# Linear attention and a gated feed-forward layer in one kernel: numerators, cosines, W sums, v casts and x transposes at other places in a hand-written order

## Chip, cores and metric

The kernel runs on one core of a Trainium2 chip. The metric is the device time of one execution in microseconds (us); before the change the median of three runs is 320.25 us (317.77 to 322.56). Five engines work side by side, each through its own list of instructions in order: TensorE (PE; its weight loads are listed as PEld), VectorE (DVE), ScalarE (ACT), GpSimd (POOL) and SyncE (SP). SP does nothing here but issue DMA transfers. An instruction waits on semaphores for the data and buffers that it needs, and everything behind it on the same engine waits with it.

## The reference

```python
batch, n_heads, seq, head_dim = 8, 8, 576, 64
theta = pi / 2 * arange(seq) / seq
def phi(x):                       # 64 -> 128 features
    r = maximum(x, 0)
    return concatenate([r * cos(theta), r * sin(theta)], axis=-1)
kv  = einsum('bhsf,bhsd->bhfd', phi(k), v)
z   = phi(k).sum(axis=2)
num = einsum('bhsf,bhfd->bhsd', phi(q), kv)
den = einsum('bhsf,bhf->bhs', phi(q), z)[..., None] + 1e-6
x   = (num / den).transpose(0, 2, 1, 3).reshape(4608, 512)
out = (gelu(x @ w_gate) * (x @ w_val)) @ w_out     # 512 -> 1536 -> 512
```

## The kernel before, in words

The attention works on batches b = 0 to 7 (576 tokens each, 4.5 tiles of 128), the feed-forward layer on blocks n = 0 to 8 of 512 tokens. The two are laid into each other: while PE multiplies block n, the attention of batch n+1 is finished and batch n+2 is loaded and prepared. The scheduler of the framework is switched off (`manual_schedule`), so each engine runs its instructions in the order in which the Python code emits them. Semaphores follow from the regions of tiles that are read and written.

**Attention of a batch.** q, k and v come from DRAM as fp32 into `st`, three slots of which q and k take the first two (`stage`, L84). For the late batches each of q and k comes in two loads: j = 0 to 3, and j = 4 to 8 (`LOADS`, L915; j counts nine groups of tokens). A *prep* makes relu(x) times cosine or sine for one j as bf16 into `phis`: `prep` for one of q, k; `prep_both` (L183) for both at once, on DVE or on ACT. `cast_v` (L207) turns v into bf16 in `vx`. `turn_q` (L220) transposes phi(q) with two DMA transposes issued from SP into the single tile `qT`, so it has to wait until the last numerators of the batch before have read `qT`. `kv_unit` (L264) multiplies phi(k) with v. `nm_unit` (L309), the *numerators* of a tile t of 128 tokens, are eight PE matmuls from `qT` into PSUM banks 6 and 7, and three DVE steps (L322 denominator, L323 reciprocal, L324 product) that write `x_sb`. `turn_x` (L375) transposes `x_sb` into `xT` of a block, again by DMA from SP.

**Feed-forward.** Blocks 0 to 3 use plain matmuls: `gv_unit` (L420) makes gate and value of 128 of the 1536 columns in PSUM, ACT takes the gelu (L439), DVE the product (L442) into `hT`. From block 4 on, gate and value are made with seven products instead of eight (class `Pair`, L639). These need sums of weights S1 to S4 (`w_sum`, L609, into `ws`) and sums of x, T1 to T4 (`x_sum`, L618, on POOL). In blocks 4 and 5 a `group` (L700) makes one `Pair` and one `gv_unit`; from block 6 on `fast_step` (L721) runs a new pair and the end of the pair before. In a `Pair`, in the order of a group:

- `p1`: four + four matmuls of 128x256 into the bank `sum`; ACT copies it to the bank `other` (L669), which must be free of the pair before (its L695).
- `p5`: into bank 3 (`MIX`); ACT copies it (L673).
- `p6`: goes on in `sum`; it has to wait for L669. DVE adds (L677) into `MIX`.
- `p2`: into `other`, then a gelu (L682). `p3`: into `MIX`, then a gelu (L686).
- `p7`: goes on in `sum`; DVE adds (L690) and multiplies (L691).
- `p4`: goes on in `sum`, which L690 must have read; DVE multiplies (L695).

The output product of block n-1 runs beside block n in one step per slot: `o_step` (L963) emits one or two of seven `product`s (L538) of six matmuls each, with copies on ACT (L565), sums on DVE (L560), and the sums of h on DVE or POOL (`h_sum`, L529). Finished rows are collected in `stores` and issued on SP by `flush` (L455), at every third step and inside `product`.

**What sets the order around the change.** Three places:

1. The list `order` (L855) between blocks 0 and 1, with its entries `("w", ...)` for the sums S2 and S4.
2. The loop over n = 1 to 3 and the steps jt = 0 to 11 (L982). In a step come: gate and value, the output step with its stores, turns of x, numerators, the preps and casts of `COMING` (L901), loads, and further sums.
3. Blocks 4 to 8, where `slot(n, jt)` (L1097) emits the output step, then `attention(n, jt)` (L1071), then the sums of `MORE`. A group g of blocks 4 and 5 holds slots 3g, 3g+1 and 3g+2: the first between p5 and p6, the second between p2 and p3, the third inside the `gv_unit`, between its gate half and p4. `PREPS` (L1059) says which preps of batch n+2 go into which slot: a letter c or C for cosine and s for sine, a capital for DVE, else ACT, and the digit j. `numerators` (L1065) says in which slots of block n the tiles of batch n+1 come; it is called after p1, after p6 and, with the third slot, ahead of p4.

On SP the end of block 3 emits `turn_q(5)`, and slot (4, 0) emits the loads of j = 4 to 8 of q and k of batch 6 behind it. In the same way slot (4, 11) emits `turn_q(6)`, and slot (5, 0) the second halves for batch 7.

## Time and profile before

The profiled execution took 318.62 us; its span from the first to the last instruction is 316.8 us. TensorE's granted clock was 0.999 on average.

| | before |
|---|---|
| median of 3 runs | 320.25 us (317.77 to 322.56) |
| profiled execution, span | 318.62 us, 316.8 us |
| PE first product of block 4, of block 5, of block 6 | 150.37, 181.91, 215.45 us |
| POOL busy, 50 to 140 us | 0.00 us |
| PE busy, 130 to 140 us | 7.88 of 10 us |
| DMA transposes of q on SP (`turn_q`), six pairs from 63.70 to 218.15 us | 8.15 to 9.15 us of issue each |
| v cast of 128x1152, DVE and POOL | 0.78 and 1.24 us (mean) |
| cosine prep of q and k together on DVE, shortest and longest | 0.47 and 1.95 us |
| sine or cosine prep of q and k together on ACT | 0.72 us (median) |
| W sum of 128x1024 on DVE | 0.68 us |

How to read it: rows of the timeline give the start in us from the beginning of the span, the duration, the engine (a q behind the name means its sequencer: issuing a transfer, not computing), the line of the kernel, the operation, what is written and read, the shape and the count of instructions in the row; in brackets, how long the engine sat idle before it and what ended that. Rows of waits give who waited for whom, the us in total, how often, and the longest. Busy is a share of the span. A busy PE is not a PE at its peak: a matmul of 128x512 shows as about 0.38 us, while the next one starts 0.216 us after it.

### The profile page before, as it was taken

The numbers are of one execution on the slowest core, as the hardware profiler recorded it, in microseconds if no ns is written. First come the engines' busy times: TensorE is split into PE (matmuls) and PEld (weight loads), VectorE is DVE, ScalarE is ACT, GpSimd is POOL, SyncE is SP. The second block draws the span as 40 slices with busy tenths as digits, with TensorE's granted clock in tenths as the row PEclk, the third lists the DMA queues.
The fourth block names the chain that finished last, engine by engine and source line by source line (L and its number), as shares of the span: only waits on it lengthen the run. The fifth ranks groups of instructions, "written<-read, shape, count | busy, mean of one in ns | idle before, by whom it ended". The sixth has DMA issues, their size and how long they took to land.

```text
span 316.8 us, 7876 instructions
## 1 busy us (share of the span) xinstructions
PE 300.1 (95%) x3055; PEld 223.2 (70%) x3055; DVE 236.8 (75%) x513; ACT 189.5 (60%) x395; POOL 135.7 (43%) x116
## 2 busy tenths in 40 slices
PE   8799998999999999979999989999999999999994
PEld 3574455645876678645777767777889888888883
DVE  5755896899898897669578856996678877757782
ACT  7764774965464754178576748674645555565631
POOL 6675440000000000007865568655994587097420
PEclk9999999999999999999999999999999999999999
DMA  7999999974699979996799899536941403113035
GB/s 269 239 177 235 319 307 397 286 107 70 185 225 182 307 220 133 298 318 176 115 211 275 246 210 168 172 66 80 153 90 37 85 10 68 33 35 66 2 75 127
DMA packets 71125, 53.66 MB, mean 169 GB/s; under 512 B 45392, under 2 KB 58448, under 8 KB 71088
## 3 DMA queue, kind: packets, MB, share of 16 engines
q1 hardware_dynamic: 61312, 41.17, 56.3%
q0 software_dynamic: 9696, 11.93, 16.5%
q8 instruction: 24, 0.39, 0.5%
q14 instruction: 13, 0.11, 0.1%
q10 hardware_dynamic: 80, 0.07, 0.1%
HBM read 37.75 MB, written 9.44 MB: 149 GB/s over the span
## 4 chain that ended last, share of the span: by engine, by line
PE 49%; DMA 24%; DVE 10%; ACT 6%; issue 6%; POOL 1%; SPq 1%; POOLq 0%; ACTq 0%; DVEq 0%
PE ps L650 18%; PE ps L547 14%; PE ps L430 13%; DMA st<-in_q_dram 6%; DMA qT<-phis 5%; DMA wo_sb<-in_moe_w_out_dram 4%; DMA wg_sb<-in_moe_w_gate_dram 2%; DMA st<-in_v_dram 2%; DMA xT<-x_sb 2%; DVE x_sb L324 2%; PE ps L270 2%; DMA wv_sb<-in_moe_w_val_dram 2%; PE ps L311 2%; DVE ps L690 2%; DVE hT L691 2%
## 5 line engine op out<-in xcount | busy, mean ns | idle before, releaser
L430 PE MATMUL ps<-xT,wg_sb 128*128 128x512 bf16 (+1 forms) x256 | 57.2, 346 | 0.7 <-DMA xT<-x_sb 0.5
L430 PE MATMUL ps<-xT,wv_sb 128*128 128x512 bf16 (+1 forms) x256 | 57.2, 346 | 0.3 <-DVE hT L442 0.3
L630 POOL TENSOR_TENSOR fs<-xT 128x512 bf16<-128x512 bf16 x10 | 12.2, 1225 | 98.9 <-DVE x_sb L324 98.0
L439 ACT ACTIVATE gel<-ps 128x512 f32<-128x512 f32 (+1 forms) x64 | 33.8, 530 | 26.6 <-PE ps L430 24.2
L442 DVE TENSOR_TENSOR hT<-gel,ps 128x512 bf16<-128x512 f32 (+1 forms) x64 | 38.0, 601 | 14.5 <-PE ps L430 12.7
L529 POOL TENSOR_TENSOR sm<-hT 128x768 bf16<-128x768 bf16 x20 | 32.8, 1641 | 30.3 <-PE ps L650 15.3
L430 PEld LDWEIGHTS <-wv_sb 128*128 128x128 bf16 x256 | 25.0, 98 | 20.6 <-issue 0.5
L547 PEld LDWEIGHTS <-sm 128*128 128x128 bf16 x336 | 32.7, 98 | 6.3
L650 PE MATMUL ps<-fs,ws 128*128 128x256 bf16 x240 | 34.6, 273 | 2.4 <-ACT ps L669 2.4
L650 PEld LDWEIGHTS <-ws 128*128 128x128 bf16 x320 | 30.5, 98 | 7.9 <-ACT ps L669 2.5
L560 DVE TENSOR_TENSOR o_sb<-sm,ps 128x256 f32<-128x256 f32 x56 | 23.4, 417 | 14.8 <-ACT sm L565 14.1
L177 ACT ACTIVATE phis<-st,sin_t 128x256 bf16<-128x256 f32 (+1 forms) x75 | 31.5, 484 | 4.6 <-DMA st<-in_q_dram 3.8
L430 PEld LDWEIGHTS <-wg_sb 128*128 128x128 bf16 x256 | 23.4, 98 | 15.3 <-DMA xT<-x_sb 0.7
L690 DVE TENSOR_TENSOR ps<-fs,ps 128x512 f32<-128x512 f32 x26 | 18.1, 695 | 19.4 <-PE ps L650 14.0
L650 PE MATMUL ps<-xT,wg_sb 128*128 128x256 bf16 x208 | 31.2, 273 | 0.0
L547 PEld LDWEIGHTS <-hT 128*128 128x128 bf16 x288 | 27.9, 98 | 4.5
L682 ACT ACTIVATE gel<-ps 128x512 f32<-128x512 f32 x26 | 15.5, 597 | 24.6 <-PE ps L650 24.5
L324 DVE TENSOR_TENSOR x_sb<-ps,rec 128x512 bf16<-128x512 f32 x38 | 26.3, 692 | 1.3
L565 ACT COPY sm<-ps 128x256 f32<-128x256 f32 x42 | 15.6, 372 | 16.2 <-PE ps L547 15.8
L547 PE MATMUL ps<-wo_sb,hT 128*128 128x256 bf16 x192 | 23.7, 273 | 0.0
L547 PE MATMUL ps<-wo_sb,sm 128*128 128x256 bf16 x168 | 22.9, 273 | 0.0
L547 PE MATMUL ps<-T,sm 128*128 128x256 bf16 x168 | 22.9, 273 | 0.0
(123 smaller groups left out, 561.7 us busy)
## 6 DMA issues: line engine op xcount, KB each, us to landing
out_dram<-o_sb SPq DMA_DIRECT2D x69, 128.0 KB, 2.5
st<-in_v_dram SPq DMA_DIRECT2D x12, 576.0 KB, 7.6
st<-in_k_dram SPq DMA_DIRECT2D x8, 576.0 KB, 5.0
st<-in_q_dram POOLq DMA_DIRECT2D x4, 576.0 KB, 12.3
st<-in_q_dram SPq DMA_DIRECT2D x4, 576.0 KB, 6.0
st<-in_q_dram SPq DMA_DIRECT2D x3, 640.0 KB, 4.5
st<-in_q_dram SPq DMA_DIRECT2D x3, 512.0 KB, 4.0
wg_sb<-in_moe_w_gate_dram POOLq DMA_DIRECT2D x6, 256.0 KB, 7.3
```

The lines of the kernel that those rows point to most:

```text
L177: nc.scalar.activation(o, i, AF.Relu, scale=tab[:, j:j + 1])
L324: nc.vector.tensor_tensor(x, nm[:, :, :, 0:D], rec[:, :, :, None].to_broadcast([128, 2, 4, D]), op=ALU.mult,)
L430: nc.tensor.matmul(bank(to[g])[:, 0:w], lhsT=wt[:, ct, js], rhs=xt[:, ct, c0:c0 + w], start=(ct == 0), stop=(ct == CT - 1),)
L439: nc.scalar.activation(gel[:, 0:w], bank(to[0])[:, 0:w], AF.Gelu)
L442: nc.vector.tensor_mul(hT[n][:, jt, c0:c0 + w], gel[:, 0:w], bank(to[1])[:, 0:w])
L529: eng.tensor_tensor(a[name][:, j0:j1], a[x][:, j0:j1], a[y][:, j0:j1], op=op)
L547: nc.tensor.matmul(at, lhsT=hs.setdefault(key, h_parts(n, p))[a][:, j], rhs=ts[b][:, j], start=(j == 0 and i in ((1, 2, 4, 5), (1, 4, 5))[ ...
L560: nc.vector.tensor_tensor(o, got[key, k], x, op=op)
L565: nc.scalar.copy(got[key, k], of)
L650: nc.tensor.matmul(to[:, 256 * half:256 * half + 256], lhsT=w_part(a, j * 128, (j + 1) * 128)[:, ct], rhs=xb[self.n][b][:, ct], start=(hal ...
L682: nc.scalar.activation(self.gel0, self.other, AF.Gelu)
L690: nc.vector.tensor_tensor(bank(val), self.m5, self.sum, op=ALU.add)
```

## The change

It computes the same and moves work. In the order of the code:

- Group 0 of blocks 4 and 5 emits, behind its `gv_unit`, the preps of a new slot 12.
- The W sums S2 and S4 (four halves, DVE) leave the list between blocks 0 and 1 and go to steps 3 to 6 of block 3.
- k of batch 5 is loaded in step (2, 10) instead of (2, 11), so ahead of `turn_q(4)`. The preps of q and k of batch 5 begin in step 7 of block 3 instead of 5 and end in step 11 instead of 10.
- In blocks 2 and 3, `turn_x` comes ahead of the output step and its stores.
- The v casts of blocks 2 and 3 go from DVE to POOL.
- `PREPS`: all cosines on DVE now lie in slot 4 (C2, C3, C4) and slot 12 (C0, C1); C5, C7 and C8 of before become c5, c7 and c8 on ACT.
- `numerators`: slots 6, 7, 9, 10 and slot 0 of the next block, in place of 5, 7, 8, 10, 11. They then lie after p1 or after p6 alone. Those of batch 7 begin two slots later.
- `turn_q(6)` and `turn_q(7)` go from slot 11 to slot 0 of the next block, behind the last numerators of the batch before and their turn, and ahead of that slot's loads.

```diff
         gv_unit(n, 8 + g, to=(2, 2), between=between)
+        if g == 0:
+            preps(n, 12)
...
-        + [("q8", 2), ("o", 1, 4), ("w", "S2", 0), ("o", 2, 4), ("kv",), ("q2", 0, 2)]
-        + [("o", 3, 4), ("w", "S2", 512)]
+        + [("q8", 2), ("o", 1, 4), ("o", 2, 4), ("kv",), ("q2", 0, 2)]
+        + [("o", 3, 4)]
...
-        + [("q2", 2, 3), ("w", "S4", 0), ("o", 2, 8), ("xt", 1, 5), ("nm", 3, 6), ("q2", 3, 4)]
-        + [("w", "S4", 512), ("o", 3, 8)]
+        + [("q2", 2, 3), ("o", 2, 8), ("xt", 1, 5), ("nm", 3, 6), ("q2", 3, 4)]
+        + [("o", 3, 8)]
...
-            5: [("qk", 5, js(0, 1))], 6: [("qk", 5, js(1, 2))], 7: [("qk", 5, js(2, 4))],
-            8: [("v", 5, 0), ("qk", 5, js(4, 5))], 9: [("v", 5, 2), ("qk", 5, js(5, 7))],
-            10: [("qk", 5, js(7, 9))],
+            7: [("qk", 5, js(0, 2))], 8: [("v", 5, 0), ("qk", 5, js(2, 4))],
+            9: [("v", 5, 2), ("qk", 5, js(4, 6))], 10: [("qk", 5, js(6, 8))],
+            11: [("qk", 5, js(8, 9))],
...
-        (2, 11): [(5, "k")], (3, 0): [(5, "q")], (3, 1): [(5, "v")],
+        (2, 10): [(5, "k")], (3, 0): [(5, "q")], (3, 1): [(5, "v")],
...
+            i = jt - t_nm - 1
+            if n > 1 and 0 <= i < late_of(b):
+                turn_x(b, i)
             if n > 1:
                 o_step(n, jt)
...
-
-            i = jt - t_nm - 1
-            if n > 1 and 0 <= i < late_of(b):
-                turn_x(b, i)
...
-                    cast_v(c, what, what + 2, dve_copy)
+                    cast_v(c, what, what + 2, nc.gpsimd.tensor_copy)
...
+            if n == 3 and 3 <= jt < 7:
+                w_sum(("S2", "S2", "S4", "S4")[jt - 3], (1 - jt % 2) * 512, (2 - jt % 2) * 512)
...
-        2: "s0 c0", 3: "s1", 4: "C1", 5: "s2 c2", 6: "s3 C3", 7: "s4", 8: "c4 s5",
-        9: "C5 s6", 10: "c6", 11: "s7 C7 s8 C8",
+        2: "s0 s1", 3: "s2", 4: "C2 C3 C4", 5: "s3 s4", 6: "c5", 7: "s5",
+        8: "c6 s6", 9: "s7", 10: "c7", 11: "s8 c8", 12: "C0 C1",
...
+    def preps(n, jt):
+        b = n + 1
+        if 4 <= b < B - 1:
+            for what in PREPS.get(jt, "").split():
+                eng = nc.vector if what[0] == "C" else nc.scalar
+                prep_both(b + 1, "cs".index(what[0].lower()), int(what[1]), eng)
+
     def numerators(n, jt):
-        b, t = n + 1, {5: 0, 7: 1, 8: 2, 10: 3, 11: 4}.get(jt)
-        if t is not None:
+        b, t = n + 1, {6: 0, 7: 1, 9: 2, 10: 3, 0: 4}.get(jt)
+        if jt == 0:
+            b = n
+        if t is not None and b > 4:
             nm_unit(b, t)
             turns.append((b, t))
...
         if n > 5:
-            i, b = n * JT + jt - 6 * JT - 5, B - 1
+            if (n, jt) == (6, 0):
+                numerators(n, jt)
+            i, b = n * JT + jt - 6 * JT - 7, B - 1
...
         b = n + 1
+        if jt == 0 and 5 < b < B:
+            turn_q(b)
...
-            if jt == 11:
-                turn_q(b + 1)
```

## The prediction

> **What bounds the kernel now.** I read the page first, then the two views of waits, then the timeline from 38 to 250 us. The page's busy list says that TensorE (PE) is the bound:

> ```profile
> PE 300.1 (95%) x3055; PEld 223.2 (70%) x3055; DVE 236.8 (75%) x513; ACT 189.5 (60%) x395; POOL 135.7 (43%) x116
> ```

> Its work is the same after the change, so only its idle stretches can be won. Busy time hides part of them, since a matmul counts as busy until its modelled end. I therefore take a gap from starts: the next start, minus the start of the group before it, minus its count times the undisturbed spacing (0.216 us for 512 columns, 0.109 for 256). Example: six matmuls of 256 from 136.83 leave PE free at 137.49, the next starts at 139.77, a gap of 2.28. After 50 us the gaps are (place, us): 52.21 1.56; 57.56 0.18; 74.34 0.39; 113.95 0.71; 120.56 0.49; 137.49 2.28; 147.69 0.31; 151.25 0.39; 164.60 0.31; 167.74 0.52; 183.43 1.12; 197.52 0.31; 200.66 0.52; 210.88 0.62; 216.97 0.68; 229.99 0.81. Together 11.2 us: no edit after 50 us can bring more.

> The largest, in the timeline, with the wait behind it:

> ```profile
> 135.95 0.72 ACT L191 ACTIVATE phis<-st,sin_t 128x512 bf16<-128x512 f32 x1 [5.12 <-DMA st<-in_q_dram]
> 136.83 0.82 PE L547 MATMUL ps<-wo_sb,sm 128*128 128x256 bf16 x6
> 139.77 0.42 PE L311 MATMUL ps<-kv_sb,qT 128*128 128x65 bf16 x8 [2.12 <-DVE x_sb L324]
> ```

> ACT and DVE sit in order behind a prep whose q had not landed; the gelu, the product with it and the numerators behind them come late, and PE last. In blocks 4 and 5 it is a chain of small waits:

> ```profile
> ACT ps L669 <- DVE hT L695: 10.1, 6, 2.2
> PE ps L650 <- ACT ps L669: 2.4, 5, 1.0
> ```

> The numerators' three DVE steps and cosines sit ahead of L695 at a group's end, so the copy L669 and the next group's third product wait.

> The stretch that decides, block 4, whose first product starts at 150.37:

> ```profile
> 152.26 9.15 SPq L222 DMA_TRANSPOSE qT<-phis  x2
> 161.46 0.59 SPq L98 DMA_DIRECT2D st<-in_q_dram  x1
> 162.09 0.50 SPq L98 DMA_DIRECT2D st<-in_k_dram  x1
> 162.33 1.64 POOL L529 TENSOR_TENSOR sm<-hT 128x768 bf16<-128x768 bf16 x1
> 162.89 1.36 DVE L193 TENSOR_SCALAR phis<-st,cos_t 128x512 bf16<-128x512 f32 x1
> 164.18 0.68 DVE L690 TENSOR_TENSOR ps<-fs,ps 128x512 f32<-128x512 f32 x1
> 164.91 0.60 PE L650 MATMUL ps<-fs,wv_sb 128*128 128x256 bf16 x4
> ```

> SP issues in order: the second halves of q and k of batch 6 (j 4 to 8) go out only after 9.15 us of transposes. The DMA view of that stretch gives the time from issue to landing:

> ```profile
> st<-in_k_dram SPq DMA_DIRECT2D x1, 640.0 KB, 5.8
> ```

> So k's second half is there at 167.9 (for block 5: issued 194.89, 5.7 us, 200.6). Before the change the first prep that reads them is s4 in slot 7, at 171.16: hidden. The cosine C1 at 162.89 took 1.36 us, not its 0.48, because POOL's step ran until 163.97; the product p4 then waited for L690.

> **The change, part by part.**

> *W sums off the first boundary.* Four DVE steps L616 of 0.68 us go. One (51.99) stands ahead of the numerators whose x_sb ends at 53.71 and frees PE at 53.77; the cosines before it wait for q until 51.46 and end at 52.07. So 0.6 of the 1.56 gap goes, the rest is q's landing. The third stands ahead of the 0.18 gap, which goes. Gain 0.8.

> *v casts to POOL.* Six casts of 0.76 us leave DVE and cost POOL 1.14 to 1.35 each (its four casts of now). POOL is idle from 50 to 140 us. The 0.49 gap at 120.56 waits for a product with gelu right behind such a cast and goes. A POOL step can hold DVE's preps up by about 0.9 (1.36 against 0.48); six of them are 0 to 5 us of DVE time, most of it beside PE. I charge 0.1: gain 0.4. In steps 8 and 9 of block 3 the casts stand among POOL's four x sums (from 144.02, waiting for xT); the sums end 1.2 later, but their xT comes some 2 us earlier, since its turn waited for the x_sb behind the 2.28 gap.

> *k of batch 5 loaded at step 10, its preps from step 7.* Now k goes out at 125.58, behind the transposes of 117.12 (8.42 us), and q at 128.82 lands 7.0 later. After, k goes out behind the store of 112.63, at about 113.8; the transposes start at about 115.5, q goes out at 125 and lands by 132, over 3 us before step 7 (135.1) asks. The 2.28 gap goes. ACT then has three preps of about 0.61 in each of steps 7 to 10, beside a gelu of 0.48 and at most one copy (2.3 to 2.6, against PE's 2.65): it ends about 0.3 late. Gain 2.3 with the 0.31 at 147.69.

> *W sums in block 3.* Four times 0.68 on DVE in steps 3 to 6, each behind the step's other work. DVE's steps then sum to 3.05, 2.35, 2.86 and 3.4 us against PE's 2.4, 2.4, 2.65 and 3.3; it trails by about 1 us, and the alternating PSUM banks allow more. Cost between 0 and 2.7 (work is added, so no gain); I take 0, since DVE was idle 4.5 of the ten us from 130.

> *x turned ahead of stores.* On SP a turn passes one pair of stores (1.1 to 1.3 us). The 0.71 gap at 113.95 waits for the turn issued at 107.98, in a step that has no store to pass: it stays. Stores end later and nobody waits. Zero; if a tile of o were still in flight it would cost the 0.6 of the one such wait (DVE L560 on out_dram).

> *Numerators between early products.* Each brings DVE 0.16+0.20+0.69. After p1, they end about 2.1 us into the group, just ahead of the next numerators (2.2) and of L677. At the end L691, L695 and L669 follow each other without them, and the cosines of slots 6, 9 and 11 are gone too. The gaps 0.52, 1.12, 0.52, 0.62, 0.68 go: 3.5. The two of 0.31 go with C1: 0.6. For batch 7 two slots (4.6 us) later, while its transposes start some 4.3 later: 0.81 at 229.99 goes.

> Gains together: 0.8+0.4+2.3+3.5+0.6+0.8 = 8.4.

> *C2 C3 C4 in slot 4, s4 in slot 5.* Their slot is three earlier for j = 4, and the load is not. DVE takes C4 ahead of L690, and p4 overwrites what L690 reads. Block 4: the last preps of q move from step 10 to 11, the transposes start about 1.6 us after the block's first product (now 1.9); k lands 1.6+9.15+0.65+5.8 = 17.2 in, C4 (0.48) and L690 (0.70) follow, p4 at 18.45. Undisturbed it starts at 164.34-150.37 = 13.97 (the numerators at 163.69, 0.26, have moved). Stall 4.5. Block 5: the transposes now stand behind the numerators of (5,4) and their turn: DVE free at 0.95, 1.05 for the three steps, 1.25 for the turn on SP, start at 3.4 (now 185.11-181.91 = 3.2). k lands at 3.4+9.1+0.65+5.7 = 18.85, p4 starts at 20.1 instead of 197.52-1.12-181.91 = 14.5. Stall 5.6. Behind C4 on DVE stand L690, L691, a sum of the output, L695 and L442, and PE waits for the first of them. Behind s4 on ACT stands L669 of the next group, due 1.75 us after p4: s4 ends before. Loss 10.1; with the shortest and the longest landing of these loads (3.8 and 8.5 us) 6.2 and 15.5. Not below 0: no load is read before it lands.

> *PE's clock.* The start shows what a cold PE costs: the first 22 matmuls of 512 took 7.03 us where 4.9 are usual, so 2.1 lost. The longest gap later, 2.28, cost nothing after it. When it falls again shows only the end, where the last matmul ended at 312.14:

> ```profile
> 315.00:316.00 1.00, 0.00 (x0) 0.00 (x0) 0.00 (x0) 0.00 (x0) 0.00 (x0) 1.00 0.00 0
> 316.00:317.00 1.00, 0.00 (x0) 0.00 (x0) 0.00 (x0) 0.00 (x0) 0.00 (x0) 0.72 0.00 0
> ```

> About 4.2 us idle before the granted clock drops (the number after the five busy times). The stalls are 4.3 and 5.5 counted from a matmul's end: the second passes it, the first is on the edge. I charge one spell, 2.1 (bounds 0 and 4.2).

> [...]

> Sum: 10.1-8.4+2.1 = 3.8 on the profiled execution's 318.62 (span 316.8): 322.4. The median of the runs is 320.25, 1.6 above that execution: 324.0.

> **Rivals.**

> *The loads are there (faster).* If the second halves land before slot 4, only the gains remain: 320.25-8.4 = 311.9. Six of six such transposes held SP for 8.2 to 9.2 us, and the loads stand behind them in both kernels; it would take a landing 4 to 5 us earlier. 0.12.

> *Both stalls cool the clock (slower).* Place: p4 in group 1 of blocks 4 and 5; price 2.1 each; it decides from about 4.2 us of idle PE. 320.25+1.7+4.2 = 326.2, at the upper bound of no change. For: 4.3 stands right at that edge. Against: one observed drop only. 0.25.

> *DVE becomes the bound in block 3.* If the W sums come onto the path, 2.7 us: 326.7. For: 3.4 against 3.3 us in step 6. Against: DVE still waits for PE there, at 125.53 for 1.46 us. 0.10.

> **How the numbers follow.** The forecast has 0.53: 324.0, between 322 without a cold spell and 326. The range 318 to 330 takes in the two slow rivals and both ends of the loads' landing (320.1 and 329.4), and leaves out the first rival and some tail. A measurement here tells 2%, 6.4 us: under 313.9 is the first rival, 0.11; over 326.6 are half of the two slow ones and the forecast's tail, 0.28; the rest 0.61.

> **What would show it.** DVE's L193 in group 1 of blocks 4 and 5 with an idle of 2 to 5 us on st<-in_k_dram or in_q_dram, and PE's L650 there waiting for L690: right. These waits absent: the first rival. The 2.28 and 1.12 gaps gone, L669 no longer on L695: the gains. Granted clock under 1.00 after 163 and 200 us: the cold spells. New gaps from 128 to 140 us: the third rival. Wrong altogether: PE's gaps in blocks 4 and 5 neither shorter nor longer.

## The result, and the profile after

The change makes the kernel slower: 327.69 us median of four runs (326.5 to 328.68) against 319.38 us for the kernel before (317.77 to 322.56, four runs beside them); the ratio is 1.0276, 95% interval 1.0202 to 1.035. Ratios compare the means of fast runs alone; the run of 322.56 counts as a slow one and is left out of this one. The profiled execution took 328.52 us, its span is 326.5 us, and the mean granted clock of TensorE 0.98. The forecast was 324.0 us with a range from 318 to 330: the sign of its sum and its range held, its point is 3.7 us low, and it had given "within 2%" the largest chance. As a change, 3.8 us were forecast and 8.3 measured.

The page of the changed kernel, the busy line and the granted clock in 40 slices of the span:

```profile
PE 303.0 (93%) x3055; PEld 224.7 (69%) x3055; DVE 236.3 (72%) x507; ACT 190.3 (58%) x395; POOL 141.0 (43%) x122
...
PEclk9999999999999999999968999799999999999998
```

PE has the same 3055 matmuls, yet is busy 2.9 us longer: some ran at a lower clock, in the slices with 6, 8 and 7, near 167, 175 and 208 us. The view of waits (who waits for whom: total us, times, longest) names the same two places:

```profile
PE ps L650 <- DVE ps L690: 11.0, 2, 5.6
...
DVE phis L193 <- DMA st<-in_k_dram: 7.5, 2, 4.1
ACT phis L191 <- DMA st<-in_k_dram: 7.5, 2, 3.9
...
PE ps L311 <- DVE x_sb L324: 2.3, 2, 1.6
```

The first line did not exist before. The waits of L669 for L695 (10.1 us before) are gone; in their place DVE and ACT wait for k, and PE behind DVE. The last line stood at 2.1 us before, for the one gap of 2.28 in block 3; that one is gone, and the line is now two new waits in block 2, taken up with experiment 7. In the timeline of block 4:

```profile
152.40 9.17 SPq L222 DMA_TRANSPOSE qT<-phis  x2
...
162.16 1.76 DVE L193 TENSOR_SCALAR phis<-st,cos_t 128x512 bf16<-128x512 f32 x2
162.24 0.52 SPq L98 DMA_DIRECT2D st<-in_k_dram  x1
...
167.97 0.72 ACT L191 ACTIVATE phis<-st,sin_t 128x512 bf16<-128x512 f32 x1 [3.61 <-DMA st<-in_k_dram]
167.99 0.49 DVE L193 TENSOR_SCALAR phis<-st,cos_t 128x512 bf16<-128x512 f32 x1 [4.07 <-DMA st<-in_k_dram]
168.39 0.69 DVE L690 TENSOR_TENSOR ps<-fs,ps 128x512 f32<-128x512 f32 x1
...
169.13 1.01 PE L650 MATMUL ps<-fs,wv_sb 128*128 128x256 bf16 x4 [5.36 <-DVE ps L690]
...
169.94 1.91 PE L430 MATMUL ps<-xT,wv_sb 128*128 128x512 bf16 x4
```

Read from the top: SP is held by the transposes of q for 9.17 us, then issues the second half of k at 162.24. C2 and C3 are made from 162.16. C4 has to wait until 167.99, L690 comes behind it, p4 behind L690. The four matmuls at 169.94 show 1.91 us where four of this kind show 1.03 at full clock. Block 5 repeats this, with C4 at 206.90 and p4 at 208.04.

The windows of the changed kernel (length, busy time of PE, PEld, DVE, ACT and POOL with instruction counts, granted clock, DMA share, GB/s):

```profile
166.00:167.00 1.00, 0.00 (x0) 0.00 (x0) 0.00 (x0) 0.00 (x0) 0.00 (x0) 0.75 1.08 376
...
168.00:169.00 1.00, 0.00 (x0) 0.00 (x0) 1.00 (x2) 0.70 (x1) 0.00 (x0) 0.50 1.03 373
...
172.00:173.00 1.00, 1.00 (x13) 0.80 (x12) 0.64 (x1) 0.26 (x1) 0.00 (x0) 0.50 0.29 64
173.00:174.00 1.00, 1.00 (x11) 0.82 (x9) 0.75 (x3) 0.54 (x2) 0.00 (x0) 0.84 0.35 72
```

A mean of 0.75 is half a microsecond at 0.5, so the clock fell at 166.50 and, by the 0.84, came back at 173.33. Such a stretch at half clock is called a cold spell. In the same way it was low from 207.46 to 210.88 (0.73 in the microsecond from 207, 0.56 in that from 210).

Gaps of PE, counted from starts as in the prediction, give the balance of the two profiled executions:

| | forecast, us | measured, us |
|---|---|---|
| gaps near 52 to 74 us (W sums) | -0.8 | -0.7 (1.56, 0.18, 0.39 become 1.16, 0, 0.23) |
| blocks 2 and 3, 100 to 150 us (casts, earlier k) | -2.7 | -0.6 (0.71, 0.49, 2.28 are gone, 0.29, 0.85, 1.75 are new; 0.31 stays) |
| blocks 4 to 6, numerators and cosines | -4.9 | -4.9 (the eight gaps from 164 to 230 us gone) |
| p4 waits for C4, block 4, block 5 | +4.5, +5.6 | +5.5, +5.8 |
| cold clock | +2.1 | +3.5 (4.2 and 2.8 us of work at half clock, half of it lost) |
| sum | +3.8 | +8.6 |

The last matmul starts 9.3 us later, the execution takes 9.9 us longer. Of what goes beyond 8.6, 0.3 us lies in the first 50 us; the rest is not assigned.

### The profile page after: what moved, and what is told of

It reads as the page before. It is cut to its first block, busy times and chain, and to the rows that moved or that the text cites. A ratio compares the mean times of both kernels' runs of the same rounds, so it can differ in the third digit from the quotient of the medians.

```text
span 326.5 us, 7887 instructions
## 1 busy us (share of the span) xinstructions
PE 303.0 (93%) x3055; PEld 224.7 (69%) x3055; DVE 236.3 (72%) x507; ACT 190.3 (58%) x395; POOL 141.0 (43%) x122
## 4 chain that ended last, share of the span: by engine, by line
PE 54%; DMA 19%; DVE 8%; SPq 6%; issue 6%; ACT 4%; POOL 1%; POOLq 0%; DVEq 0%; ACTq 0%
PE ps L650 22%; PE ps L547 14%; PE ps L430 12%; DMA st<-in_q_dram 6%; SPq L222 5%; DMA wo_sb<-in_moe_w_out_dram 4%; DMA st<-in_k_dram 4%; DMA st<-in_v_dram 3%; DMA qT<-phis 2%; PE ps L311 2%; DVE phis L179 2%; PE ps L270 2%; DVE hT L442 1%; ACT phis L177 1%; SPq L98 1%
## 5 line engine op out<-in xcount | busy, mean ns | idle before, releaser
L430 PE MATMUL ps<-xT,wv_sb 128*128 128x512 bf16 (+1 forms) x256 | 58.9, 354 | 0.0
L208 POOL CAST vx<-st 128x1152 bf16<-128x1152 f32 x10 | 12.1, 1211 | 92.8 <-PE ps L430 66.9
L442 DVE TENSOR_TENSOR hT<-gel,ps 128x512 bf16<-128x512 f32 (+1 forms) x64 | 37.9, 599 | 17.6 <-PE ps L430 14.1
L529 POOL TENSOR_TENSOR sm<-hT 128x768 bf16<-128x768 bf16 x20 | 32.8, 1641 | 23.1 <-PE ps L650 17.5
L547 PEld LDWEIGHTS <-sm 128*128 128x128 bf16 x336 | 32.9, 98 | 7.1 <-issue 0.4
L650 PE MATMUL ps<-fs,ws 128*128 128x256 bf16 x240 | 34.7, 274 | 0.2 <-ACT ps L669 0.2
L560 DVE TENSOR_TENSOR o_sb<-sm,ps 128x256 f32<-128x256 f32 x56 | 23.4, 418 | 15.6 <-ACT sm L565 14.6
L650 PEld LDWEIGHTS <-ws 128*128 128x128 bf16 x320 | 30.3, 98 | 4.3 <-ACT ps L669 0.5
L690 DVE TENSOR_TENSOR ps<-fs,ps 128x512 f32<-128x512 f32 x26 | 18.1, 695 | 20.0 <-PE ps L650 13.7
L547 PEld LDWEIGHTS <-hT 128*128 128x128 bf16 x288 | 28.2, 98 | 5.4
L650 PE MATMUL ps<-xT,wg_sb 128*128 128x256 bf16 x208 | 31.8, 276 | 0.0
L682 ACT ACTIVATE gel<-ps 128x512 f32<-128x512 f32 x26 | 15.5, 597 | 26.4 <-PE ps L650 26.4
L324 DVE TENSOR_TENSOR x_sb<-ps,rec 128x512 bf16<-128x512 f32 x38 | 26.3, 691 | 1.3
L650 PE MATMUL ps<-fs,wv_sb 128*128 128x256 bf16 x104 | 16.4, 283 | 11.0 <-DVE ps L690 11.0
L179 DVE TENSOR_SCALAR phis<-st,cos_t 128x256 bf16<-128x256 f32 x62 | 21.1, 389 | 5.6 <-DMA st<-in_q_dram 5.6
L529 POOL TENSOR_TENSOR sm<-hT,sm 128x768 bf16<-128x768 bf16 x10 | 16.4, 1641 | 17.8 <-PE ps L547 15.4
```

Of the source, the lines that this page charges most:

```text
L179: (eng or nc.vector).tensor_scalar(o, i, 0.0, tab[:, j:j + 1], op0=ALU.max, op1=ALU.mult)
L324: nc.vector.tensor_tensor(x, nm[:, :, :, 0:D], rec[:, :, :, None].to_broadcast([128, 2, 4, D]), op=ALU.mult,)
L430: nc.tensor.matmul(bank(to[g])[:, 0:w], lhsT=wt[:, ct, js], rhs=xt[:, ct, c0:c0 + w], start=(ct == 0), stop=(ct == CT - 1),)
L442: nc.vector.tensor_mul(hT[n][:, jt, c0:c0 + w], gel[:, 0:w], bank(to[1])[:, 0:w])
L529: eng.tensor_tensor(a[name][:, j0:j1], a[x][:, j0:j1], a[y][:, j0:j1], op=op)
L547: nc.tensor.matmul(at, lhsT=hs.setdefault(key, h_parts(n, p))[a][:, j], rhs=ts[b][:, j], start=(j == 0 and i in ((1, 2, 4, 5), (1, 4, 5))[ ...
```

## Experiments

The runs of before beside the experiments have medians of 320.55, 320.42, 320.92 and 320.72 us in the four sets. In each trace of the experiments 23 matmul records are missing; the gaps of 0.22 us at these places are not counted.

**1. Where the first load is cut.** j = 4 comes with the first load of q and k; the order of preps stays.

```diff
-        (3, 9): [(6, "q", 0, 4), (6, "k", 0, 4)],
-        (4, 0): [(6, "q", 4, R), (6, "k", 4, R)], (4, 1): [(6, "v")],
-        (4, 8): [(7, "q", 0, 4), (7, "k", 0, 4), (7, "v")],
-        (5, 0): [(7, "q", 4, R), (7, "k", 4, R)]
+        (3, 9): [(6, "q", 0, 5), (6, "k", 0, 5)],
+        (4, 0): [(6, "q", 5, R), (6, "k", 5, R)], (4, 1): [(6, "v")],
+        (4, 8): [(7, "q", 0, 5), (7, "k", 0, 5), (7, "v")],
+        (5, 0): [(7, "q", 5, R), (7, "k", 5, R)]
```

> The changed kernel, only that the first loads of q and k for batches 6 and 7 carry j = 0 to 4 instead of 0 to 3 (and the second ones j = 5 to 8). No instruction of DVE, ACT or PE moves. Theory: the two long gaps of TensorE are DVE's wait for j = 4, which stood in the second loads behind the transposes of q. Then the gaps of 5.5 and 5.8 us fall under 0.5 us each, the granted clock stays at 1.00, and with 3.5 us of cold matmuls gone the time falls by about 14 us, from 327.7 to 313 to 316. Rival: three cosines in one slot (with POOL's steps beside them) are too much for DVE there. Then gaps of 1.5 us or more stay in both places, and the time falls by less than 10 us.

Measured: 316.69 us (315.12 to 319.01), ratio to before 0.990 (0.983 to 0.997), 11.0 us under the changed kernel, the clock at 1.00. That is a little short of the theory's 313 to 316, and half of the rival is there too. PE's waits from 140 us on:

```profile
PE ps L650 <- DVE ps L690: 3.3, 2, 2.1
```

Two gaps stay at p4, 1.36 and 2.25 us, with all data there: three cosines in one slot, beside POOL's steps, are more than DVE has room for (in the changed kernel the two of C2 and C3 take 1.76 us there in block 4 and 2.65 in block 5, against 0.48 for one alone). The sum agrees: 5.5 + 5.8 of stalls and 3.5 of cold clock go, 3.6 stay, so 11.2 should be won and 11.0 are. So the wait for the load is the loss, and this version is 1% below the kernel before.

**2. The stall kept, PE kept busy.** Twenty matmuls whose result nobody reads stand ahead of p4 in group 1 of blocks 4 and 5.

```diff
             z()
+            if g == 1:
+                dummies(20, 7)
             f.p4()
```

> The changed kernel with 20 matmuls of 512 columns of old data into PSUM bank 7 just ahead of p4 in group 1 of blocks 4 and 5 (4.3 us of TensorE work inside gaps of 5.5 and 5.8 us; nothing reads their result). Theory: the granted clock falls because TensorE idles, and costs 2.1 us after the first gap and 1.4 us after the second. Then the clock stays at 1.00 through both places, DVE's wait for the loads is as long as before, and the time falls by 3 to 4 us to about 324. Rival: the clock has another cause, or matmuls after a wait are slow anyway: the clock falls as before and the time stays within 1 us of 327.7, or rises.

Measured: 324.65 us (321.99 to 324.86), ratio 1.0124 (1.0058 to 1.0189), 3.0 us under the changed kernel. The mean granted clock of the profiled execution is 0.996, against 0.980 in the changed kernel. The timeline shows that p4 starts as late as before, and the matmuls of 512 behind it at full clock:

```profile
163.22 4.48 PE L157 MATMUL ps<-ws 128*128 128x512 bf16 x20
...
167.51 0.49 DVE L193 TENSOR_SCALAR phis<-st,cos_t 128x512 bf16<-128x512 f32 x1 [3.98 <-DMA st<-in_k_dram]
...
168.66 0.60 PE L650 MATMUL ps<-fs,wv_sb 128*128 128x256 bf16 x4 [0.96 <-DVE ps L690]
...
169.09 1.03 PE L430 MATMUL ps<-xT,wv_sb 128*128 128x512 bf16 x4
```

The same four matmuls of 512 show 1.03 us here and 1.91 us above. The two cold spells cost 3.0 us in the medians, against 3.5 read from the trace.

**3. Only C4 moved, s4 stays on ACT in slot 5.**

```diff
-        4: "C2 C3 C4",
+        4: "C2 C3",
...
-        9: "s7"
+        9: "C4 s7"
```

> The changed kernel with the cosine of j = 4 moved from slot 4 to slot 9 (still on DVE); the sine of j = 4 stays on ACT in slot 5. Theory: p4 of group 1 no longer waits, and ACT, held by the sine until k lands, passes the wait on to the copy L669 of the next group: TensorE then stands at p6 of group 2 instead, for 1.5 to 3 us in each block, under the idle time at which the clock fell; about 318. Rival: ACT's wait is covered; no gap over 0.5 us in either place and about 314.

Measured: 315.31 us, in one run only, clock 1.00. ACT hands the wait on, as the timeline shows:

```profile
164.04 0.72 ACT L191 ACTIVATE phis<-st,sin_t 128x512 bf16<-128x512 f32 x1 [3.22 <-DMA st<-in_k_dram]
...
165.30 0.60 PE L650 MATMUL ps<-fs,ws 128*128 128x256 bf16 x4 [1.01 <-ACT ps L669]
```

PE loses 1.18 us in block 4 and 1.07 in block 5 for s4, somewhat less than the 1.5 to 3 expected. C4 is the expensive one, since DVE's L690 stands directly behind it and directly ahead of p4.

**4. The second loads ahead of the transposes on SP.** At the end of block 3 and in slot 0 of block 5 the loads go out first, `turn_q` follows.

```diff
             if (n, jt) == (3, JT - 1):
+                start_loads(4, 0)
                 turn_q(b + 1)
...
         if jt == 0 and 5 < b < B:
+            start_loads(n, jt)
             turn_q(b)
...
-        start_loads(n, jt)
+        if jt:
+            start_loads(n, jt)
```

> The changed kernel, only that SP issues the second loads of q and k (batches 6 and 7) just ahead of the transposes of q instead of behind them. Theory: the loads were late because of the 9 us for which SP issues transposes. Then k's second half lands 8 to 9 us earlier, both gaps go, the clock stays at 1.00, and the time is 313 to 316; the transposes start about 1.2 us later and end just before the numerators of slot 6. Rival: the landing is set by the DMA engines, which carry the transposes at the same time: the issue is earlier and the landing is not; 325 or more.

Measured: 317.52 us (315.98 to 317.83), ratio 0.9911 (0.9856 to 0.9965), against 313 to 316 expected. No prep waits for a load any more, so the 9 us of transposes are what made k late. p4 again has 1.36 and 2.25 us, and the numerators of slot 6 wait 0.53 us for qT. This run also has a cold spell that the profiled run of experiment 1 lacks; the windows around the gap that begins at 194.63 show it:

```profile
195.00:196.00 1.00, 0.00 (x0) 0.00 (x0) 1.00 (x2) 0.99 (x2) 0.55 (x1) 1.00 0.99 141
...
197.00:198.00 1.00, 1.00 (x8) 0.61 (x7) 1.00 (x3) 0.00 (x0) 0.00 (x0) 1.00 0.73 120
198.00:199.00 1.00, 1.00 (x6) 0.54 (x5) 0.82 (x2) 0.00 (x0) 0.00 (x0) 0.50 0.93 201
```

The clock falls at 198.00, after 2.25 us of idle PE and more than a microsecond after PE has gone on. The gap of the same length in experiment 1, from 195.26, cost no clock, as two rows of its trace show (the p4 that ends the gap, and the window behind it):

```profile
197.51 0.60 PE L650 MATMUL ps<-fs,wv_sb 128*128 128x256 bf16 x4 [2.09 <-DVE ps L690]
...
198.00:199.00 1.00, 1.00 (x8) 0.52 (x6) 1.00 (x3) 0.00 (x0) 0.00 (x0) 1.00 1.04 382
```

**5. The kernel before with nothing but an early C4.**

```diff
-    4: "C1", ... 8: "c4 s5",
+    4: "C1 C4", ... 8: "s5",
```

> The kernel before with one thing of the change: the cosine of j = 4 on DVE in slot 4 (with C1) instead of on ACT in slot 8. Theory (k's second half lands at 167.9 and 200.6, and that is the whole loss): p4 of group 1 waits 4.0 to 4.5 us in each of blocks 4 and 5 and the granted clock falls for one or two spells, 1.4 to 3.5 us: 10 to 12 us more than before, about 331. Rival 1 (the loss needs s4 on ACT in slot 5 too, whose copy L669 is late): under 5 us more, below 325.5. Rival 2 (the clock holds): 8 to 9 us more, about 329.

Measured: 334.46 us (332.75 to 335.57), ratio 1.0441 (1.0374 to 1.0508): 14.0 us more for one prep put four slots earlier and on DVE instead of ACT. Its waits:

```profile
PE ps L650 <- DVE ps L690: 9.9, 2, 5.6
...
DVE phis L193 <- DMA st<-in_k_dram: 8.6, 2, 4.9
...
ACT ps L669 <- DVE hT L695: 4.0, 2, 2.2
```

The gaps of p4 are 4.50 and 5.71 us, 9.6 more than the two of 0.31 that were there; the clock is low twice, for 3.41 and 6.83 us. So C4 by itself, without the rest of the change, makes the whole loss, and its price is above the 10 to 12 us that were expected. The rest of the change thus takes back 6.8 us (334.46 less 327.69).

**6. The order of preps of before in the changed kernel.** All else of the change is kept.

```diff
-        2: "s0 s1", 3: "s2", 4: "C2 C3 C4", 5: "s3 s4", 6: "c5", 7: "s5",
-        8: "c6 s6", 9: "s7", 10: "c7", 11: "s8 c8", 12: "C0 C1",
+        2: "s0 c0", 3: "s1", 4: "C1", 5: "s2 c2", 6: "s3 C3", 7: "s4", 8: "c4 s5",
+        9: "C5 s6", 10: "c6", 11: "s7 C7 s8 C8",
```

> The changed kernel with the order of the preps of before (C4 on ACT in slot 8, s4 in slot 7), all its other parts kept. Theory (the other parts gain what they were charged less 2 us in blocks 2 and 3, and the preps' order is the whole loss): no wait of L193 on a load, the granted clock 1.00, about 6.8 us under before (the difference between the run with only C4 moved and the changed kernel): 313.0 to 314.5. Rival 1 (all gains as predicted): 8.4 under before, 312.0. Rival 2 (the gains in blocks 4 and 5 need the cosines away from the group ends as well): the numerators of slot 6 wait 0.5 to 2 us for qT or gaps of 0.5 to 1 stay at the group ends, 315.5 to 317.

Measured: 315.0 us (312.88 to 315.81), ratio 0.9803 (0.9737 to 0.9869), 5.9 us under the runs of before beside it. It lies between the theory's 313.0 to 314.5 and rival 2's 315.5 to 317. No prep waits for a load. Gaps of 0.57 twice at p4, 0.45 and 1.40 stay in blocks 4 and 5, the last of them for a reason that the timeline of this run shows:

```profile
206.35 2.12 POOL L616 TENSOR_TENSOR st<-wv_sb 128x1024 bf16<-128x1024 bf16 x1
206.39 2.37 DVE L193 TENSOR_SCALAR phis<-st,cos_t 128x512 bf16<-128x512 f32 x1
...
209.42 0.60 PE L650 MATMUL ps<-xT,ws 128*128 128x256 bf16 x4 [1.24 <-DVE ps L677]
```

One cosine of 0.48 us takes 2.37 beside a W sum on GpSimd, the product behind it is late, and PE waits.

**7. The casts of v in blocks 2 and 3 back on DVE**, in the changed kernel, and **8.** the same in the kernel of experiment 6.

```diff
-                    cast_v(c, what, what + 2, nc.gpsimd.tensor_copy)
+                    cast_v(c, what, what + 2, dve_copy)
```

> The changed kernel with the six casts of v in blocks 2 and 3 back on DVE. Theory (GpSimd's casts slow DVE's cosines in that stretch): the three L179 behind the landing of v4 take about 0.9 us again instead of 2.50, the gap of 1.75 us at about 114.6 shrinks to the 0.7 of before, and the gap of about 0.49 near 120.5 is back; together 0.3 to 0.8 us less, about 327.0 against 327.7. Rival (the slow L179 comes from something else, such as the landing loads): L179 still takes over 1.8 us and the gap stays over 1.2.

> The changed kernel with the order of the preps of before and the casts of v in blocks 2 and 3 on DVE: what stays is numerators between early products, the earlier load of batch 5, the W sums in block 3 and the turns of x ahead of the stores. Theory (GpSimd's casts cost by slowing DVE's cosines, and cover nothing that DVE lacks): the 0.85 us wait of the numerators on x_sb near 114 is gone, about 0.5 near 120 is back, 0 to 1 us less than with the casts on GpSimd: 314.0 to 315.0, ratio to before 0.978. Rival (DVE needs the relief, as the change assumes): gaps over 0.5 us on DVE's products in blocks 2 and 3, 316 or more.

Measured: 327.83 us (326.31 to 328.88), ratio 1.0233 (1.016 to 1.0306), for the first, against 327.69; 314.73 us (312.97 to 315.21, six runs), ratio 0.9815 (0.9765 to 0.9864), for the second, against 315.0. The casts make no difference that these runs can tell. The trace still shows the effect. In the changed kernel, block 2:

```profile
111.62 1.15 POOL L208 CAST vx<-st 128x1152 bf16<-128x1152 f32 x1 [18.57 <-DMA st<-in_v_dram]
...
111.82 2.50 DVE L179 TENSOR_SCALAR phis<-st,cos_t 128x256 bf16<-128x256 f32 x3
...
116.34 0.42 PE L311 MATMUL ps<-kv_sb,qT 128*128 128x65 bf16 x8 [1.58 <-DVE x_sb L324]
```

With the casts on DVE (experiment 7) the three cosines take 0.87 us, and the numerators find `x_sb` free. What PE then waits for is the transposed x:

```profile
112.93 0.87 DVE L179 TENSOR_SCALAR phis<-st,cos_t 128x256 bf16<-128x256 f32 x3
...
113.99 0.61 PE L430 MATMUL ps<-xT,wg_sb 128*128 128x256 bf16 x4 [0.50 <-DMA xT<-x_sb]
...
168.08 1.01 PE L650 MATMUL ps<-fs,wv_sb 128*128 128x256 bf16 x4 [6.51 <-DVE ps L690]
```

The gap is 0.66 us in place of 1.75, the 0.50 near 120 is back, and so at most 0.6 us was at stake. In the six traces with the casts on POOL these cosines take 1.60 to 2.50 us, but in only four of them do the numerators then wait for `x_sb` (1.75 us three times, 0.84 in experiment 6). Two limits lie together at this place: in experiment 9, with the casts on DVE, the wait for xT makes a gap of 1.76 us, where the row of four transposes of x ahead of it on SP lasts 6.56 us instead of the 5.58 of experiment 7. The other new gap, 0.29 + 0.85 us at 107 to 108, stands behind the load of q of batch 4. It is there in experiments 1, 2, 6 and 10 too, with casts on either engine, and goes with that load's landing: the sines that wait for it on ACT start at 104.65 to 105.61 us in these four and the changed kernel (105.61), and at 102.70 to 104.59 in four traces without the gap, of before and of experiments 3, 4 and 7 (103.96).

What experiment 7 wins in block 2 it loses again: its block 4 starts 2.2 us earlier than in the changed kernel (147.43 against 149.64), but p4 there, the last row above, ends a gap of 6.68 us instead of 5.52, and the mean granted clock is 0.975 instead of 0.980. While p4 waits for k, time won ahead of it can be lost at p4.

**9. and 10. Two spreads of the cosines**, both with the cut after j = 4 and the casts on DVE: C4 in slot 9, and C2, C3 at the end of group 1 with C4 at the end of group 2.

```diff
-        4: "C2 C3 C4", ... 9: "s7", ... 12: "C0 C1",
+        4: "C2 C3", ... 9: "C4 s7", ... 12: "C0 C1",
...
+        5: "s3 s4", ... 12: "C0 C1", 13: "C2 C3", 14: "C4",
...
-        if g == 0:
-            preps(n, 12)
+        preps(n, 12 + g)
```

> The changed kernel with the first loads of batches 6 and 7 cut after j = 4 instead of j = 3, the cosine of j = 4 moved from slot 4 to slot 9, and the casts of v in blocks 2 and 3 on DVE. Theory (late loads, two cosines too many in one group, and the cast are all that was lost): p4 of group 1 has gaps under 0.8 us in blocks 4 and 5, the clock stays at 1.00, block 2 and 3 gaps fall to 0.7 + 0.5; 4 to 5 us below the 316.7 that the cut after j = 4 gave alone: 311 to 313, ratio to before 0.975. Rival (the remaining gaps come from the numerators between the early products, which stay): gaps over 1.2 us in group 1, 315 to 317.

> As the run before this one, but with the cosines C2 and C3 at the end of group 1 and C4 at the end of group 2, none in slot 4 or 9. Theory (cosines cost where they share a group with the numerators, and nothing at a group's end): no gap over 0.4 us in blocks 4 and 5, 310 to 312, some 1 us below the run before. Rival (cosines at a group's end bring back the waits of before, 0.5 to 1.1 us at each): two to four gaps of 0.5 to 1.1, 313 to 315.

Measured: 323.56 us (322.21 to 324.9), ratio 1.0105 (1.0043 to 1.0167), and 324.34 us (323.45 to 326.46), ratio 1.0139 (1.0074 to 1.0205). Neither theory nor rival: both kernels put C4 of batch 6 behind slot 8, whose load for batch 7 now writes over j = 4. The cosine of j = 4 of batch 6 is therefore made from the data of batch 7, and it waits for that load, as the timeline of the first shows:

```profile
181.89 0.49 DVE L193 TENSOR_SCALAR phis<-st,cos_t 128x512 bf16<-128x512 f32 x1 [5.35 <-DMA st<-in_k_dram]
...
183.04 0.60 PE L650 MATMUL ps<-xT,ws 128*128 128x256 bf16 x4 [4.79 <-DVE ps L677]
```

So these two kernels do not compute what the reference does, and their times say nothing about a spread of the cosines. A prep has an earliest slot, the landing of its load, and a latest one, the load that takes its place; the cut after j = 4 shifts both.

**11. C4 in slot 7, 12. s4 in slot 7 and C4 in slot 9.** The first with the cut after j = 4, the second with the loads of the changed kernel, both with the casts on DVE.

```diff
-        4: "C2 C3 C4", 5: "s3 s4", ... 7: "s5", ... 9: "s7"
+        4: "C2 C3", 5: "s3 s4", ... 7: "C4 s5", ... 9: "s7"
+        4: "C2 C3", 5: "s3", ... 7: "s4 s5", ... 9: "C4 s7"
```

> As the run with C4 in slot 9 and the cut after j = 4, but with C4 in slot 7, ahead of the load of slot 8 that writes over j = 4. Theory: all preps read what they should and wait for nothing; p4 gaps near 1.0 and 1.9 us as there, numerators of slot 6 of block 4 wait 1.3 us for qT, the rest gone, 312.5 to 314.5. Rival (a third wait appears in group 2 where C4 now stands): 315 or more.

> The changed kernel with its own loads, but s4 in slot 7 and C4 in slot 9, behind the landing of the second halves (about 167.9 and 200.6), and the casts of v in blocks 2 and 3 on DVE. Theory (only the two preps of j = 4 were early; moving them is enough): no wait of L193 or L191 on a load, the 0.96 to 1.18 us that ACT passed on when s4 stayed are gone, 312.5 to 314.5. Rival (s4 in slot 7 holds up L669 there as it did in slot 5): waits of 0.5 to 1.2 us, 315 to 316.

Measured: 317.4 us (316.33 to 317.74), ratio 0.9882 (0.9823 to 0.9941); and 316.27 us (315.42 to 316.93), ratio 0.9859 (0.979 to 0.9928). Both missed the expected 312.5 to 314.5, and the rivals are right in kind. In the first, p4 of group 2, where C4 now stands, waits 0.68 us in block 4 and 0.27 in block 5. In the second no wait for a load holds PE up any more, but p4 of group 2 waits 0.68 us twice, since the gelu L686 now stands behind two sines on ACT. More is lost in group 1, with only two cosines in slot 4: 0.98 and 1.85 us at p4 in the first, 0.99 and 1.85 in the second. The timeline of the second run in block 5:

```profile
191.84 1.64 POOL L529 TENSOR_TENSOR sm<-hT 128x768 bf16<-128x768 bf16 x1
...
192.40 2.65 DVE L193 TENSOR_SCALAR phis<-st,cos_t 128x512 bf16<-128x512 f32 x2
...
193.42 1.35 POOL L208 CAST vx<-st 128x1152 bf16<-128x1152 f32 x1
...
195.70 0.60 PE L650 MATMUL ps<-fs,wv_sb 128*128 128x256 bf16 x4 [1.69 <-DVE ps L690]
```

Two cosines of 0.48 us each take 2.65 us beside POOL's sum and cast. With the order of preps of before (experiments 6 and 8) p4 loses 0.57 in both blocks: cosines gathered in slot 4 are no gain even when their data are there.

## Why the forecast held in kind and missed in size

- **k's second half reaches C4 too late: right, a little short.** Forecast 4.5 and 5.6 us, measured 5.5 and 5.8. In block 4 the step that failed is "the transposes start about 1.6 us after the block's first product": they start 2.76 us after it (152.40 and 149.64). The timeline of the changed kernel shows why:

```profile
150.33 1.63 POOL L529 TENSOR_TENSOR sm<-hT 128x768 bf16<-128x768 bf16 x1 [1.04 <-PE ps L650]
150.50 1.75 DVE L193 TENSOR_SCALAR phis<-st,cos_t 128x512 bf16<-128x512 f32 x1
...
152.40 3.48 SPq L222 DMA_TRANSPOSE qT<-phis  x1
```

  The last cosine of q, now in step 11, meets a POOL step and takes 1.75 us; before the change the last one took 0.47, at 150.85. The transposes, the loads behind them and C4 all move with it, by 1.2 us, and the stall is 1.0 longer than forecast.
- **C2, C3 and C4 beside POOL's step: a term that was put at nothing.** The prediction had seen POOL hold up one cosine in that place (1.36 us) and charged nothing for three. Experiments 1 and 4, where no load is late, still show gaps of 1.36 and 2.25 us at p4, 3.6 together against 0.6 before. In the changed kernel the longer wait for k hides them.
- **One cold spell, 2.1: mis-sized by 1.4.** There were two, 3.5 us by the trace and 3.0 by experiment 2. The prediction read a threshold of 4.2 us idle off the end of the kernel and put block 4 "on the edge". That 4.2 was one sample, no threshold: in experiment 4 a spell followed 2.25 us of idle PE (see the last section). The second rival, both stalls cool the clock, is what happened, though its price of 4.2 was 0.7 too high; with 326.2 us it is 1.5 below the median.
- **Blocks 2 and 3, 2.7: 0.6 came, the term that was mis-sized most.** The 2.28 and the 0.49 went as said; the 0.31 at 147.69, which was to go with them, stayed (146.96). "I charge 0.1" for DVE held up by POOL's casts was too little: one group of three cosines took 1.6 us longer. But experiments 7 and 8 show no difference in time without it; the wait for xT, which the prediction left at 0.71, and the landing of q of batch 4 stand at the same place. How much of the 2.1 missing is the cast and how much the queue of that execution stays open.
- **Numerators, group ends, block 6, 4.9: right to 0.1 us** in the changed kernel. Experiment 6 shows that a part is given back when the cosines return to their old slots.
- **W sums, 0.8 and nothing in block 3: right** (0.7; no new gap in steps 3 to 6 of block 3). The third rival did not occur. **The first rival**, the loads are there, fell with the waits for k.

The gains together are 6.2 us by gaps; 6.8 by experiment 5 against the changed kernel, 5.9 by experiment 6 against before. The 8.4 of the forecast was about 2 us too much, the loss 2.6 too little. Both errors point the same way, so the change came out at more than twice the 3.8 us forecast. That the point is only 3.7 us low is in part luck: it was added to a median of 320.25 us for the kernel before, and the four runs beside the changed kernel have 319.38.

## What to carry to other kernels

When a step is moved earlier, follow its data back to the issuing queue and read what that queue does before: here 9 us of transposes on SP decided, and one cosine of 0.48 us, put four slots earlier and on DVE, cost 14 us. When a load is cut elsewhere instead, look at its other end too, the next load into the same place. Before a prep is counted at its best time, look for a GpSimd step beside it (a cosine of 0.48 us took 2.37 in experiment 6), and where a stall is forecast, ask where it lies and not only how long it is: 2.25 us of idle PE were followed by a cold spell in experiment 4 and by none in experiment 1.

## What the runs showed of the hardware

*DVE beside GpSimd.* A cosine of 128x512 takes 0.47 to 0.49 us alone, 1.75 beside a sum of h (1.63) and 2.37 beside a W sum (2.12) on POOL; three of 128x256 take 0.87 alone and 2.50 beside casts. The cosines of 1.75 and 2.37 us, in the changed kernel and in experiment 6, both end 0.29 us after the POOL step beside them (152.25 after 151.96, 208.76 after 208.47).
